# Wider weight pieces before the main loop, a resident last weight chunk, and coupled remainders in an attention + GLU block on one Trainium2 core

## The chip, the cores and the metric

The kernel runs on one core of a Trainium2 chip (trn2). The metric is the device time of one launch in microseconds (us). Engines are named as the profile names them: PE multiplies matrices (PEld is its weight load), DVE, ACT and POOL work on rows of elements, SP issues the DMAs. Each engine works through its own queue in order; engines wait for each other by semaphores.

## What is computed

One transformer block on 2048 rows of 512 numbers: a layer norm with a modulation computed from `c`, attention with 32 heads of 16 numbers that share one key and one value head, a second modulated norm, and a gated linear unit with 1792 hidden columns. Cut to what matters:

```python
mod = (silu(c) @ w_mod).reshape(1, 6, 1, -1)          # sa, ca, ga, sb, cb, gb
h = layernorm(x) * (1 + ca) + sa
q = h @ wq  (32 heads of 16);  k = h @ wk;  v = h @ wv    # one k and v for all heads
p = softmax(q k^T / 4);  x = x + ga * ((p v) @ wo)
h = layernorm(x) * (1 + cb) + sb
x = x + gb * ((sigmoid(h @ w_gate) * (h @ w_up)) @ w_down)
```

## The kernel before

**Numbers.** Most products are made from float16 pairs: a value is split into a high part and the rest, and a product is three passes (high x high, high x low, low x high). So every weight has to be read as float32, scaled, and split into two float16 halves before it is used.

**Three stages in time.** First a prologue, whose order is the hand-written list `PLAN` (a token is one small step: `a` is one score tile for the row maxima, `x` its reduction on DVE, `q` a part of a query projection, `jb` one "beat" of the weight jobs, `mx`, `mn`, `mz` the end of unit 0's row maxima). Then a main loop of 32 units of 16 steps; a unit is 128 query rows and 16 heads, and two units make one block of 128 rows (16 blocks). Last a tail with what of the feed-forward part is left over, which runs with full 128x128 matmuls and whose order a scheduler sets.

**A step of the main loop** is two half-steps. Each issues in a fixed order two transposed score tiles (`st`, whose exponential ACT writes to `P`), two score tiles for the row maxima of a unit ahead (`sa`, reduced by DVE to `mx`), one part of P times V (`craw`), and then one piece of feed-forward or query work (`piece`, pieces of some terms). All these matmuls use a quarter of the columns and half of the rows of the array (64*32); eight of them at different places run side by side. A *term* here is 8 such matmuls, two row halves times four column groups; a term of 512 columns does the work of one full 128x128 matmul.

**Feed-forward groups of a block**, in terms: the output projection `wo` (12), three pairs of gate and up of 512 hidden columns each (24 a pair), the last 256 hidden columns, gate and up together (`rest`, 12), and the down projection (42): 138. There are two ways to run a group on the two row halves:

- `Halves`: each row half of the contraction goes into a bank of its own; at the end DVE reads one bank, ACT the other, and POOL adds them.
- `Couple`: two groups share the array, each on one row half, and change sides in the middle. Each ends as one whole sum in one bank. At the change PE waits until the half that was issued before is done (`take_over`; a tiny `nought` matmul in `hand_over` counts it).

Before the change the three pairs are Couples, and `wo`, `rest` and `down` are Halves.

**Order of the groups.** When block b's units end, `wo` of block b is put into `urgent` with a first step (`SKIP` 9 steps into the next unit, `SKIP0` 5 for the first block), and `pairs[0]`, the `down` of the block before, `pairs[1]`, `pairs[2]`, `rest` into `work`. `pick` takes the next group that is ready, `pace` says how many terms a half-step gets (2 to 3), `places` spreads them.

**Weights.** Gate and up weights are split once, kept in HBM (`wD`, the last chunk in `wD1`) and read back for every block as tiles of 512 KB (`gw`, `GWB` = 7 buffers, two DMAs a tile, 14 tiles a block). `ask` puts a tile's two loads into a list when a buffer has been spent, and `drip` issues one of them, or one of the waiting transposes, each half-step. The down weights stay on chip.

Splitting is done in two places. Five of the seven chunks are split in the prologue by 20 jobs: `job_load` reads a piece of 256 KB, `job_beat` makes the two halves (two activations on ACT, one subtraction on POOL) and stores the result of two beats ago in two DMAs, and then loads the piece of two beats ahead (four pieces in flight). The rest is split in the main loop (`weight_jobs`, 26 pieces, each three operations on POOL behind a load), over the first 52 steps.

**Row maxima.** A unit's score rows are shifted by their maximum. The chain is `m` (DVE) to `mm` (ACT, then DVE) to `mt` (DVE), out to HBM and back into rows of `qp` (`mD`), and only then can the unit's first `st` run. In the prologue this chain is unit 0's.

Of the kernel before, what the change touches and what calls it, by code (L numbers as in the profile page):

```python
# [16 lines left out]
P = 128  # L17
# [46 lines left out]
SKIP, SKIP0 = 9, 5  # L64
# [25 lines left out]
GWB = 7  # L90
# [4 lines left out]
NGW = 4 * NPR + 2  # L95
JCH = 5
# [3 lines left out]
def adaln_mqa_glu_kernel(  # L100
# [649 lines left out]
    def recip(b, o, lD, rD):  # L750
# [16 lines left out]
        defer(W2 if b else 1, recip2)  # L767
# [44 lines left out]
    wD1 = dr.tile([2, P, 2, 4, 256], F16, name="wD1")  # L812
    CH = [*range(2, NCH), 0, 1]
# [6 lines left out]

    def weight_jobs():
        jobs = []
        gw = {}

        def gate_up(i, kk, m):
            if m == 0:
                gw[i, kk] = gw_tile()
            g_ = gw[i, kk].rearrange("p m (k n) -> p k m n", k=2)

            def store():  # L830
                for k in range(2):
                    dst = wD[i // 2, 2 * kk + k, :, :, i % 2 * 256:(i % 2 + 1) * 256] if i < 2 * NPR else wD1[kk, :, k]
                    sp1.dma_start(dst, g_[:, k])
                gw.pop((i, kk))
                if (i, kk) == (NCH - 1, 1):
                    ask(0)

            split_weight((w_gate, w_up)[m][2 * kk * P:2 * (kk + 1) * P, CH[i] * 256:(CH[i] + 1) * 256].rearrange("(k p) n -> p k n", p=P),
                         g_[:, :, m], g_[:, :, 2 + m], [2, 256], store if m == 1 else None)

        for i in range(JCH, NCH):
            for kk in range(2):
                for m in range(2):
                    jobs.append(lambda i=i, m=m, kk=kk: gate_up(i, kk, m))
            if i == JCH:
                for k in range(4):
                    jobs.append(lambda k=k: split_weight(wo[k * P:(k + 1) * P, :], WO['woh'][:, k], WO['wol'][:, k], [D]))
        for k in FS:
            jobs.append(lambda k=k: split_weight(w_down[k * P:(k + 1) * P, :], wdh[:, k], wdl[:, k], [D]))
        return jobs  # L850
# [20 lines left out]
    def ask(spent):  # L871
        while use[0] < min(spent + GWB, NGW * NQ):
# [3 lines left out]
            src = wD[i // NDC, i % NDC] if i < NDC * NPR else wD1[i - NDC * NPR].rearrange("p k m n -> p (k m n)").rearrange("p (m n) -> p m n", n=512)  # L876
# [4 lines left out]
    def ffn_block(b):  # L881
# [38 lines left out]
        def wo_end(pa, pb):  # L920
# [64 lines left out]
        def last_begin():  # L985
            if tail:
                ask(at + NDC * NPR)
            fetched(at + NGW - 1)

        def last_term(n, rs):  # L990
            k, i = divmod(n, 3)
            gw = gws[at + NDC * NPR + k // 2].rearrange("p m n -> p (m n)")
# [4 lines left out]
        def last_end(pa, pb):  # L997
# [29 lines left out]
        def down_end(pa, pb):  # L1027
# [18 lines left out]
        first = Halves("wo", 12, "po", wo_term, wo_end, wo_alone, wo_begin)  # L1046
        pairs = [Couple(gu_pair(p, 0), gu_pair(p, 1)) for p in range(NPR)]
        rest = Halves("gu", 12, "pgu", last_term, last_end, last_alone, last_begin)
        down = Halves("dn", 3 * NFC, "pd", down_term, down_end, down_alone)
# [3 lines left out]
        for k in range(2):  # L1053
            rest.after[6 * k + 5] = lambda spent=at + NDC * NPR + k + 1: ask(spent)
        for g in (*pairs, rest):
            g.needs = [((b, "h2"), HGAP if b else EGAP)]
        down.needs = [((b, f"g{p}"), GAP) for p in range(NPR)] + [((b, f"g{NPR}"), -99)]
        return first, pairs, rest, down, norm_alone


    jobs, beat, wst = [(i, kk, m) for i in range(JCH) for kk in range(2) for m in range(2)], [0], {}

    def job_load(k):
        i, kk, m = jobs[k]
        if k == 0:
            wst["f"] = pro.tile([P, 4, D], F32, tag="xb", name="xb", bufs=4)
            wst["h"] = pro.tile([P, 4, 2, 2, 256], F16, tag="xb", name="xb", bufs=4)
        src = (w_gate, w_up)[m][2 * kk * P:2 * (kk + 1) * P, CH[i] * 256:(CH[i] + 1) * 256].rearrange("(k p) n -> p k n", p=P)
        sp1.dma_start(wst["f"][:, k % 4].rearrange("p (k n) -> p k n", k=2), src)

    def job_store(k):
        i, kk, m = jobs[k]
        for z in range(2):
            sp1.dma_start(wD[i // 2, 2 * kk + z].rearrange("p (e m) n -> p m e n", e=2)[:, m, :, i % 2 * 256:(i % 2 + 1) * 256],
                          wst["h"][:, k % 4, :, z])

    def job_beat():
        k, beat[0] = beat[0], beat[0] + 1
        if k < len(jobs):
            w_ = wst["f"][:, k % 4]  # L1080
            hi, lo = (wst["h"][:, k % 4, e].rearrange("p k n -> p (k n)") for e in range(2))
# [29 lines left out]
    def q_end(b, o):  # L1111
# [11 lines left out]
              "la": lambda: load_q(0, 0, 1), "lb": lambda: load_q(0, 1, 2), "jl": lambda: [job_load(k) for k in range(4)], "jb": job_beat}  # L1123
# [5 lines left out]
    downs, late = [], []  # L1129
# [7 lines left out]
    WO["wol"] = P2.tile([P, 4, D], F16, name="wol")  # L1137

# [49 lines left out]
    def pace(s, g):  # L1188
        if g.stage == "q":
            return QRATE, 2  # L1190
        now_, late_ = s // (NU * NKB), s % (NU * NKB) >= CHAIN
        until = 2 * ((now_ + late_) * NU * NKB + CHAIN)
        left = sum(z.n for z in [g, *urgent, *work] if late_ or z.b < now_ - 1 or z.stage == "wo") + 12 * late_
        if until > 2 * len(units) * NKB:
            until, left = 2 * len(units) * NKB, left - 12 * late_
        return min(max(LEAST, left / max(until - 2 * s, 1)), MOST), MOST
# [39 lines left out]
    for i, (b, o) in enumerate(units):  # L1236
        if o == 0 and b > 0:
            first_, pairs_, rest_, down_, _ = ffn_block(b - 1)
            first_.ready = i * NKB + (SKIP if b > 1 else SKIP0)
            urgent.append(first_)  # L1240
            block = [pairs_[0], *downs[-1:], *pairs_[1:], rest_]
            downs.append(down_)
            for g in (first_, *block):
                g.b = b - 1
# [59 lines left out]
    left = [*urgent, *work, downs[-1]]  # L1304
# [59 lines left out]
```

## Time and profile before

| | |
|---|---|
| runs | 1670.15, 1673.82, 1676.3 us; median 1673.82 |
| the profiled execution | 1675.08 us, span in the trace 1673.3 us |
| instructions | 92934 |
| PE, DVE, ACT, POOL busy | 1581.2, 1421.7, 1303.4, 685.6 us |
| granted PE clock, mean | 0.978 |
| read from and written to HBM | 160.23 and 20.56 MB |

The profile is of one execution. An engine's busy time is the union of its instructions; matmuls are pipelined, so their durations overlap and a busy PE is not PE at its peak. In rows of a timeline the columns are start, duration, engine, line, operation, result and operands, shape and count, and in square brackets how long the engine stood idle before it and what ended that. A table of waits has the total in us, the number of waits and the longest. In a table by stretches each engine has its busy time and the number of its instructions in brackets; then follow the granted clock, the share of time that the DMA engines were busy, and what they moved in GB/s. SPq is SP's queue: the time an issue took there.

### The profile page before, as it was taken

Reading aid. Unit: us, or ns where it says so; the run is one execution under the profiler, and the core shown is the slowest. Engines: PE = TensorE matmul, PEld = TensorE weight load, DVE = VectorE, ACT = ScalarE, POOL = GpSimd, SP = SyncE. Lnnn points to the kernel's source line nnn. Section 1 sums busy time; section 2 is a strip of 40 time slices with the busy share of each in tenths; the row PEclk is TensorE's granted clock in tenths of the full one; section 3 lists DMA queues with packets and bytes.
Section 4 is the critical chain, followed back from the end, with each engine's and each line's share of the span. In section 5 each row is a group of like instructions: output and inputs, shape, how many; then the busy total and the mean of one; then the engine's idle time right before and its main releaser. Section 6 shows DMA issues by size and latency. Waiting matters only on the chain.

```text
span 1673.3 us, 92934 instructions
## 1 busy us (share of the span) xinstructions
PE 1581.2 (94%) x41818; PEld 989.8 (59%) x41818; DVE 1421.7 (85%) x2410; ACT 1303.4 (78%) x2354; POOL 685.6 (41%) x824
## 2 busy tenths in 40 slices
PE   6868988999999999999999999999999999999998
PEld 3313544656666566666666666766666666666544
DVE  7548987989999999999999999999999999998031
ACT  4655876878888788888888888888888888888821
POOL 4542557634252525244352526252524435242510
PEclk9777999999999999999999999999999999999999
DMA  6473343642615325435373545454443636353553
GB/s 204 137 200 88 100 120 111 174 109 82 169 35 145 102 70 135 119 112 141 85 164 89 126 96 139 85 138 111 125 123 100 150 85 163 88 124 93 138 191 107
DMA packets 247482, 203.86 MB, mean 122 GB/s; under 512 B 126140, under 2 KB 178092, under 8 KB 247084
## 3 DMA queue, kind: packets, MB, share of 16 engines
q1 hardware_dynamic: 247084, 197.92, 44.6%
q8 instruction: 327, 5.36, 1.3%
q14 instruction: 71, 0.58, 0.1%
HBM read 160.23 MB, written 20.56 MB: 108 GB/s over the span
## 4 chain that ended last, share of the span: by engine, by line
PE 79%; DMA 6%; DVE 5%; ACT 5%; issue 2%; SPq 1%; POOL 1%; ACTq 0%; POOLq 0%; DVEq 0%
PE craw L146 22%; PE pgu L146 17%; PE sa L146 13%; PE st L146 12%; PE pd L146 7%; DVE mx L146 3%; ACT P L146 3%; PE po L146 2%; PE pd L266 2%; PE pq L146 2%; PE pgu L203 2%; DMA qp<-mD 1%; DMA xb<-in_B_w_up_dram 1%; SPq L146 1%; DMA mD<-mt 1%
## 5 line engine op out<-in xcount | busy, mean ns | idle before, releaser
L146 DVE TENSOR_REDUCE mx<-sa 128x1 f32<-128x512 f32 x2048 | 1293.2, 682 | 103.0 <-PE sa L146 86.3
L146 ACT ACTIVATE P<-st 128x512 f32<-128x512 f32 x2048 | 1166.7, 597 | 239.0 <-PE st L146 180.3
L146 PE MATMUL craw<-P,V 64*32 64x512 f32 x8192 | 1090.3, 595 | 0.8 <-issue 0.7
L146 PE MATMUL st<-qp,kp 64*32 64x512 f16 x8192 | 841.0, 380 | 19.6 <-ACT P L146 14.1
L146 PE MATMUL sa<-kp,qp 64*32 64x512 f16 (+1 forms) x7940 | 658.8, 380 | 35.9 <-DVE mx L146 33.5
L146 PEld LDWEIGHTS <-kp 64*32 64x32 f16 x8192 | 331.9, 91 | 279.4 <-issue 106.4
L146 PE MATMUL pgu<-gw,h 64*32 64x512 f16 x9600 | 427.8, 376 | 4.0 <-issue 2.4
L146 PEld LDWEIGHTS <-qp 64*32 64x32 f16 (+1 forms) x7940 | 259.5, 93 | 134.9 <-issue 73.2
L146 PEld LDWEIGHTS <-h 64*32 64x32 f16 (+1 forms) x9792 | 214.9, 92 | 84.2 <-issue 27.7
L146 PEld LDWEIGHTS craw<-P,V 64*32 64x32 f32 x8192 | 242.9, 105 | 23.0 <-issue 8.5
L146 PE MATMUL pd<-wdh,g 64*32 64x512 f16 x2912 | 150.2, 376 | 1.1 <-issue 0.8
L980 POOL TENSOR_SCALAR th<-th 128x512 f32<-128x512 f32 (+1 forms) x57 | 32.3, 566 | 276.5 <-ACT th L146 262.1
L146 PEld LDWEIGHTS <-g 64*32 64x32 f16 x4368 | 93.7, 92 | 32.9 <-issue 9.3
L1033 POOL TENSOR_TENSOR o<-o,gb 128x512 f32<-128x512 f32 x13 | 16.7, 1283 | 211.1 <-ACT o L146 211.1
L146 PE MATMUL pd<-wdl,g 64*32 64x512 f16 x1456 | 90.1, 376 | 1.8 <-issue 1.8
L609 POOL MEMSET qp<- 32x1024 f16 x60 | 56.7, 944 | 55.3 <-PE st L146 53.0
L981 POOL TENSOR_TENSOR th<-th,u 128x512 f32<-128x512 f32 (+1 forms) x57 | 65.3, 1146 | 4.7
L146 PE MATMUL po<-woh,a 64*32 64x512 f16 x960 | 59.4, 386 | 6.6 <-POOL a L774 6.6
L908 POOL TENSOR_TENSOR rows<-th,rows 128x512 f16<-128x512 f32 (+1 forms) x57 | 59.5, 1044 | 4.6
L146 PE MATMUL craw<-nought 64*32 64x1 f16 x336 | 54.8, 163 | 0.0
L146 DVE COPY u<-pgu 128x512 f32<-128x512 f32 x43 | 29.3, 681 | 26.6 <-PE pgu L146 19.1
L146 PE MATMUL pq<-h,wdh 64*32 64x512 f16 (+1 forms) x688 | 51.0, 388 | 0.0
(163 smaller groups left out, 1105.1 us busy)
## 6 DMA issues: line engine op xcount, KB each, us to landing
gw<-wD SPq DMA_DIRECT2D x448, 256.0 KB
wm<-in_w_mod_dram SPq DMA_DIRECT2D x6, 1024.0 KB
qp<-qD SPq DMA_DIRECT2D x186, 32.0 KB
wD<-xb SPq DMA_DIRECT2D x40, 128.0 KB
qD<-q SPq DMA_DIRECT2D x16, 256.0 KB
xr<-in_A_x_dram SPq DMA_DIRECT2D x16, 256.0 KB
out_dram<-ot SPq DMA_DIRECT2D x16, 256.0 KB
rD<-cs SPq DMA_DIRECT2D x124, 32.0 KB
```

The lines of the kernel that those rows point to most:

```text
L146: return (lambda *a, **k: keep(f_(*a, **k))) if pinned else f_
L203: pe.matmul(cut[0](self.bank) if cut else self.bank, l_, r_, start=(n == 0), stop=(n == self.n - 1))
L266: pe.matmul(self.bank, *self.term(n, slice(0, P)), start=(n == 0), stop=(n == self.n - 1))
L609: eng.memset(qp[j:j + 32], 0.0)
L908: pool.tensor_tensor(rows[:, n:2 * n], src, rows[:, :n], op=ALU.subtract)
L980: pool.tensor_scalar(th, th, 1.0, 1.0, op0=ALU.add, op1=ALU.mult)
L981: pool.tensor_tensor(th, th, u_, op=ALU.mult)
L1033: pool.tensor_tensor(o2, o2, mods[5], op=ALU.mult)
```

## The change

- **Prologue.** The weight jobs become 16 (`JP` = 2 pairs of 512 columns, four row blocks, gate and up) on pieces of 128 rows by 512 columns. A piece's rows are now 2 KB in the load, where they were 1 KB, and 1 KB in the store, where they were 512 B; a store is one DMA, where it was two. Eight pieces are in flight, loaded by `jl0` and `jl1` well ahead of the first beat, and a beat loads the piece of six beats ahead. The last beats come earlier in `PLAN`, ahead of `mx` and `mn`.
- **Main loop, weights.** It splits 30 pieces, where it was 26, over the same 52 steps. The last chunk's halves go to a tile that stays on chip (`gr`, the size of two `gw` tiles), so a block reads 12 tiles back, where it was 14; `GWB` is 6.
- **Groups.** From block 2 on `wo` is coupled with the `rest` of the block before. From block 6 on the `down`s of two blocks are coupled and run two blocks later; `rest` of block 0, `wo` of blocks 0 and 1 and `down` of blocks 0 to 5 stay Halves.
- **Pace.** `pace` spreads what is left evenly over all steps that are left, where it aimed at dates in each block.
- **First block.** `SKIP0` is 7, and the reciprocal of the first block's softmax sums is issued 3 steps after the load that it needs, where it was 1.

```diff
-SKIP, SKIP0 = 9, 5
+SKIP, SKIP0 = 9, 7
+PSOLO, DSOLO = 2, 6
-GWB = 7
+GWB = 6
-NGW = 4 * NPR + 2
-JCH = 5
+NGW = 4 * NPR
+JP = 2
...
-        defer(W2 if b else 1, recip2)
+        defer(W2, recip2)
...
+        def wo_end(po, second):
...
+            t1, xr = t32("t1"), x1["x"]
+            dve.tensor_tensor(t1, po, mods[2], op=ALU.mult)
+
+            def norm():
+                pool.tensor_tensor(xr, t1, xr, op=ALU.add)
+                defer(1, norm2)
...
+        def last_end(p_, second):
...
+            th, u_ = t32("th")[:, :256], t32("u")[:, :256]
+            act.activation(th, p_[:, :256], AF.Tanh, scale=0.5 / (SH * SW))
+            act.activation(u_, p_[:, 256:], AF.Identity)
+            gated(th, u_, NPR, 256)
...
+        def down_end(pd, second):
...
+            ot = t32("ot")
+            if second:
+                act.activation(ot, pd, AF.Identity)
+            else:
+                dve.tensor_tensor(ot, pd, mods[5], op=ALU.mult)
...
     def job_beat():
...
-        if k >= 2:
-            job_store(k - 2)
-            if k + 2 < len(jobs):
-                job_load(k + 2)
+        if n >= 2:
+            job_store(n - 2)
+            if n + 6 < len(jobs):
+                job_load(n + 6)
...
+    gr = P2.tile([P, 2, 2048], F16, name="gr")
...
     def pace(s, g):
...
-        now_, late_ = s // (NU * NKB), s % (NU * NKB) >= CHAIN
-        until = 2 * ((now_ + late_) * NU * NKB + CHAIN)
-        left = sum(z.n for z in [g, *urgent, *work] if late_ or z.b < now_ - 1 or z.stage == "wo") + 12 * late_
...
+        ahead = 138 * (NQ - 2 - s // (NU * NKB))
+        left = sum(z.n for z in [g, *urgent, *work]) + ahead
+        return min(max(LEAST, left / max(2 * len(units) * NKB - 2 * s, 1)), MOST), MOST
...
+            proj, pairs_, rest_, down_, _ = ffn_block(b - 1)
+            g = proj
+            if rests:
+                g = Couple(rests.pop(), proj)
+                g.stage = "wo"
...
+            if len(downs) == (1 if b - 1 <= DSOLO else 2):
+                d = downs[0] if len(downs) == 1 else Couple(*downs)
```

ACT's queue at the end of the prologue, before the change: `xb` is one activation of a weight job, `q_` the reading of a finished query projection, `mm` the step of unit 0's chain of row maxima that stands on ACT.

```order
L146 ACTIVATE xb<-xb 128x512 x2
L146 ACTIVATE q_1061<-pq 128x512
L146 ACTIVATE q_1060<-pq 128x512
L146 ACTIVATE xb<-xb 128x512 x12
L146 ACTIVATE q_1165<-pq 128x512
L146 ACTIVATE q_1164<-pq 128x512
L146 ACTIVATE xb<-xb 128x512 x8
L146 ACTIVATE mm<-m 128x16
```

The same place after it:

```order
L147 ACTIVATE xb<-xb 128x512 x2
L147 ACTIVATE q_1061<-pq 128x512
L147 ACTIVATE q_1060<-pq 128x512
L147 ACTIVATE xb<-xb 128x512 x10
L147 ACTIVATE q_1150<-pq 128x512
L147 ACTIVATE q_1149<-pq 128x512
L147 ACTIVATE mm<-m 128x16
```

Behind the first query evictions stood 20 activations of weight jobs ahead of `mm`; now 10 do, and none between the second evictions and `mm`.

SP's queue in the same stage, before: loads of pieces (`xb<-in_`), stores of results (`wD<-xb`, two DMAs each), and the store of a finished query projection (`qD<-q_`), which waits for POOL.

```order
L146 DMA wD<-xb 256x1x256 x2
L146 DMA xb<-in_B_w_up_dram 128x2x256
L146 DMA wD<-xb 256x1x256 x2
L146 DMA xb<-in_B_w_gate_dram 128x2x256
L591 DMA qD<-q_908 128x2x512
L146 DMA wD<-xb 256x1x256 x2
L146 DMA xb<-in_B_w_up_dram 128x2x256
```

After:

```order
L147 DMA wD<-xb 256x1x512
L147 DMA xb<-in_B_w_up_dram 128x512
L592 DMA qD<-q_914 128x2x512
L147 DMA wD<-xb 256x1x512
L147 DMA xb<-in_B_w_gate_dram 128x512
```

A store is one entry, where it was two, and a load that stands behind `qD<-q_` is now for the sixth beat after it, where it was for the second.

DVE's queue in the middle of the main loop, before, about one unit from the end of one block's pairs on: `u<-pgu` reads an up half, `th<-pgu` one of the two banks of `rest`, the others belong to the attention part.

```order
L146 COPY u<-pgu 128x512
L146 TENSOR_REDUCE mx<-sa 128x1 x8
L146 RECIPROCAL rc<-lc 128x16
L146 TENSOR_REDUCE mx<-sa 128x1 x6
L146 COPY th<-pgu 128x512
L146 TENSOR_REDUCE mx<-sa 128x1 x16
L146 TENSOR_REDUCE m<-mx 128x16
L146 TENSOR_REDUCE mx<-sa 128x1 x4
L146 SCALAR_TENSOR_TENSOR mm<-m,mm 128x16
```

The same stretch of a block after:

```order
L147 RECIPROCAL rc<-lc 128x16
L147 TENSOR_REDUCE mx<-sa 128x1 x6
L147 COPY u<-pgu 128x512
L147 TENSOR_REDUCE mx<-sa 128x1 x16
L147 TENSOR_REDUCE m<-mx 128x16
L147 TENSOR_REDUCE mx<-sa 128x1 x4
L147 SCALAR_TENSOR_TENSOR mm<-m,mm 128x16
L147 STREAM_TRANSPOSE mt<-mm 128x32
```

The copy `th<-pgu` of 512 columns is gone from DVE: 14 of them in the whole program before, 1 after. DVE loses 3 more reads of a `down` bank; ACT loses 13 reads of a `wo` bank and 4 of a `down` bank; POOL's additions of two halves go with them.

Counted over both programs, PE issues the same number of terms, but not at the same place: in the main loop 9600 matmuls into `pgu` and 4368 into `pd` before, 9408 and 4032 after (8 a term: 24 and 42 terms fewer), and the tail has 24 and 42 full matmuls more. Besides the last block and the `down` before it, which the tail does in both, the loop leaves it a `down`, two pairs and a `rest` before, and two `down`s, three pairs and a `rest` after. PE issues 10 more of the tiny `nought` matmuls.

More of the change, by code (lines that the diff above doesn't have):

```diff
@@ L811, in adaln_mqa_glu_kernel @@
     wD = dr.tile([NPR, NDC, P, 4, 512], F16, name="wD")
-    wD1 = dr.tile([2, P, 2, 4, 256], F16, name="wD1")
-    CH = [*range(2, NCH), 0, 1]
+    CH = [2, 3, 4, 5, 0, 1, 6]
     FS = [2 * c_ + e for c_ in CH for e in range(2)]
@@ L1063, in job_load @@
[L1063 to L1075, printed above, removed]
+        down.needs = [((b, f"g{p}"), GAP) for p in range(NPR)] + [((b, f"g{NPR}"), GAP)]
@@ new lines, in ffn_block, with job_load, job_store @@
+        return proj, pairs, rest, down, norm_alone
+    jobs, beat, wst = [(p, k, m) for p in range(JP) for k in range(NDC) for m in range(2)], [0], {}
+    def job_load(n):
+        p, k, m = jobs[n]
+        if n % 4 == 0 and n < 8:
+            wst[n // 4] = pro.tile([P, 4, D], F32, tag="xb", name="xb", bufs=4)
+        if n == 0:
+            wst["h"] = pro.tile([P, 4, 2, D], F16, tag="xb", name="xb", bufs=4)
+        sp1.dma_start(wst[n // 4 % 2][:, n % 4], gate_up_part(p, k, m))
+    def job_store(n):
+        p, k, m = jobs[n]
+        sp1.dma_start(wD[p, k].rearrange("p (e m) n -> p m e n", e=2)[:, m], wst["h"][:, n % 4])
@@ L1077, in job_beat @@
     def job_beat():
[L1078 to L1081, printed above, removed]
+        n, beat[0] = beat[0], beat[0] + 1
+        if n < len(jobs):
+            w_ = wst[n // 4 % 2][:, n % 4]
+            hi, lo = (wst["h"][:, n % 4, e] for e in range(2))
             act.activation(hi, w_, AF.Identity, scale=SW)
@@ L1303, in adaln_mqa_glu_kernel @@
     last_unit()
-    left = [*urgent, *work, downs[-1]]
+    left = [*urgent, *work]
     assert all(g.stage in ("gu", "dn") for g in left)
-    old = [g for g in left if g.stage == "dn"]
-    left = [g for g in left if g.stage == "gu"]
     def go_on(g):
@@ L1322, in adaln_mqa_glu_kernel @@
     late.clear()
-    for g in old[:-1]:
-        g.alone()
     norm_()
     go_on(pairs_[0])
-    old[-1].alone()
+    downs[0].alone()
     for g in pairs_[1:]:
```

118 lines of the change are left out of this document (69 added, 49 removed), and 14 rows, old and new, of the table PLAN.

## The prediction

> **What bounds the kernel now.** I read the busy times first, then the stretches, then the waits of the stretches that fall off. A stretch's columns are its length, PE, PEld, DVE, ACT, POOL, clock, DMA share and GB/s; the last row, of one tile's instructions, has PE, PEld and ACT alone.
>
> ```profile
> span 1673.3 us, 92934 instructions
> ...
> PE 1581.2 (94%) x41818; PEld 989.8 (59%) x41818; DVE 1421.7 (85%) x2410; ACT 1303.4 (78%) x2354; POOL 685.6 (41%) x824
> 80.00:100.00 20.00, 18.72 (x121) 6.28 (x118) 13.32 (x23) 13.49 (x24) 9.25 (x9) 0.91 0.78 221
> 110.00:130.00 20.00, 1.15 (x5) 0.31 (x5) 1.68 (x4) 10.86 (x19) 9.38 (x9) 0.58 0.79 223
> 800.00:1200.00 400.00, 393.66 (x11710) 263.44 (x11702) 377.10 (x634) 337.19 (x611) 164.75 (x191) 1.00 0.47 115
> 800.00:1200.00 400.00, 297.78 (x2248) 68.46 (x2248) 321.46 (x562) 1.00 0.47 115
> ```
>
> The middle of the loop is full: in 400 us PE works 393.7 and DVE 377.1, so both stand near the step time. The last row is the same stretch for the exponentials and their matmuls alone: 562 exponentials, four a step, are 140.5 steps of 2.85 us. The prologue has a hole: from 110 to 130 us PE works 1.15 of 20 us and DVE 1.68, while the DMA engines are busy 0.79 of the time. The waits from 84 to 150 us and the timeline say why:
>
> ```profile
> DVE mm L146 <- ACT mm L146: 18.3, 1, 18.3
> ```
>
> ```profile
> 97.71 0.57 SPq L146 DMA_DIRECT2D xb<-in_B_w_up_dram  x1
> 102.10 0.37 SPq L591 DMA_DIRECT2D qD<-q  x1
> ...
> 108.83 0.22 DVE L146 TENSOR_REDUCE m<-mx 128x16 f32<-128x64 f32 x1
> 127.19 1.29 ACT L146 ACTIVATE xb<-xb 128x512 f16<-128x512 f32 x2 [3.66 <-DMA xb<-in_B_w_up_dram]
> 128.38 0.20 ACT L146 ACTIVATE mm<-m 128x16 f16<-128x16 f32 x1
> 128.61 1.18 DVE L146 SCALAR_TENSOR_TENSOR mm<-m,mm 128x16 f16<-128x16 f32 x1 [18.28 <-ACT mm L146]
> 130.66 8.95 PE L146 MATMUL sa<-kp,qp 64*128 64x512 f16 x15 [19.51 <-DVE mx L146]
> 139.54 0.61 PE L146 MATMUL st<-qp,kp 64*32 64x512 f16 x4
> ```
>
> The row maximum `m` is there at 108.83 us. Its next step stands on ACT behind the last weight jobs, which wait for their loads, and runs at 128.38. DVE holds its queue for 18.28 us, PE runs out of score banks for 19.51 us. The loads are late because a beat asks only two beats ahead, and because SP stands for 3.8 us (98.28 to 102.10) before a query store, with a load behind it.
>
> **Step by step, against the profiled 1675.1 us.**
>
> *1. The hole in the prologue.* With 16 jobs, eight pieces loaded before the first beat and six in flight after it, the queue position of `mm` has no load near it. Two jobs keep ACT 2.46 us:
>
> ```profile
> 73.62 2.46 ACT L146 ACTIVATE xb<-xb 128x512 f16<-128x512 f32 x4
> ```
>
> From the first job at 73.6 us to 108.8 us are 35 us; 16 jobs need 19.7 us of ACT, and in the stretch from 80 to 100 us above ACT was busy 13.5 of 20 us with the jobs and all else: it fits. So I take 18.0 of the 18.28 us, 139.54 becoming about 121.5. Ends: -5 if ACT or the stores are still behind by 13 us, -22 if the smaller ACT waits before 109 us go too.
>
> *2. First block.* Around 240 to 285 us four stretches of 5 us have PE at 9.2 of 20 us, 10.8 us lost:
>
> ```profile
> 240.00:245.00 5.00, 1.64 (x29) 0.62 (x28) 2.21 (x5) 0.97 (x3) 2.97 (x4) 0.80 0.51 172
> 250.00:255.00 5.00, 1.58 (x37) 0.54 (x35) 1.18 (x2) 0.97 (x2) 4.59 (x7) 0.83 0.71 213
> 265.00:270.00 5.00, 2.74 (x69) 1.09 (x53) 3.44 (x7) 1.99 (x5) 4.83 (x7) 1.00 0.00 0
> 280.00:285.00 5.00, 3.25 (x96) 1.58 (x87) 3.28 (x7) 2.81 (x6) 0.00 (x0) 1.00 0.29 71
> DVE rc L146 <- DMA lc<-lD: 4.2, 1, 4.2
> PE po L146 <- POOL a L774: 3.4, 1, 3.4
> POOL wst L379 <- DMA wst<-in_B_w_down_dram: 25.0, 7, 7.3
> ```
>
> The 4.2 us on DVE goes: three steps of 2.85 us cover it. The wait of `po` stays, since its operand comes two steps later and so does `wo`. POOL's waits for pieces remain, with four pieces more. I take -6, the 4.2 and some 2 of what was late behind it; ends 0 and -10.8.
>
> *3. Terms that move.* The price of a term, from the page and from the middle of the loop:
>
> ```profile
> L146 PE MATMUL pgu<-gw,h 64*32 64x512 f16 x9600 | 427.8, 376 | 4.0 <-issue 2.4
> 855.64 0.66 PE L146 MATMUL pgu<-gw,h 64*32 64x512 f16 x16
> 856.94 0.66 PE L146 MATMUL pgu<-gw,h 64*32 64x512 f16 x16
> 858.24 0.40 PE L146 MATMUL pgu<-gw,h 64*32 64x512 f16 x5
> 858.28 0.16 PE L146 MATMUL craw<-nought 64*32 64x1 f16 x1
> 858.28 0.61 PE L146 MATMUL pgu<-gw,h 64*32 64x512 f16 x11
> 859.53 0.66 PE L146 MATMUL pgu<-gw,h 64*32 64x512 f16 x16
> ```
>
> A half-step with two terms (16 matmuls of 0.38 us, eight side by side), where nothing waits, is 1.30 us, so 2.60 a step; counted in the program's order a step has 4.3 terms in blocks 5 to 15 before. The tail prices a term:
>
> ```profile
> 1600.55 1.92 PE L146 MATMUL craw<-P,V 64*32 64x512 f32 x16
> 1644.87 5.34 PE L203 MATMUL pgu<-gw,h 128*128 128x512 f16 x24
> 1648.30 2.69 SPq L878 DMA_DIRECT2D gw<-wD x6
> 1650.05 0.60 PE L899 MATMUL pt<-ident,th 128*128 128x128 f32 x4
> 1650.49 5.34 PE L203 MATMUL pgu<-gw,h 128*128 128x512 f16 x24
> ```
>
> 24 matmuls from 1644.87 to 1650.05 are 0.216 us each. In the loop 66 terms fewer save 66 x 0.216 = 14.2 us where PE is the limit, nothing where DVE is. DVE is busy 94% here; I take -14 (ends 0, -15), since the quoted half-steps run at PE's own pace.
>
> *4. Evictions.* DVE loses 16 reads of a bank and ACT 17, all in the loop. The columns are busy time and ns of one:
>
> ```profile
> L146 DVE COPY th<-pgu 128x512 f32<-128x512 f32 x11 | 7.5, 680 | 0.0
> ```
>
> 16 x 0.68 = 10.9 us of DVE. Where PE is the limit they are hidden under it; I take half, -5 (ends 0, -11). ACT and POOL, less busy, count for nothing.
>
> *5. One buffer fewer.* A pair's last two tiles can only be asked for when the pair ahead has spent its first two: 15 terms before their use, seven half-steps of 1.4 us. `drip` sends one half tile a half-step, transposes first, so counted in the planner's order the worst tiles are issued two to five half-steps ahead (2.8 to 7 us), where it was seven. In the tail row above a load issued at 1648.30 is used from about 1652.4 without a wait, so it landed within 4.1 us. Most arrive in time; I take +3 in the loop (ends 0, and 14 blocks x 1.3 us short = +18).
>
> *6. Four pieces more, ten `nought`s more, more side changes.* POOL, busy 41%, hides the pieces, three operations each:
>
> ```profile
> 137.37 0.62 POOL L379 TENSOR_SCALAR wst<-wst 128x512 f32<-128x512 f32 x1
> 138.07 1.15 POOL L381 TENSOR_TENSOR gw<-wst,gw 128x512 f16<-128x512 f32 x1
> ```
>
> That is 4 x (0.62 + 0.62 + 1.15) = 10 us of its own; if one stands before a block's `a` it costs PE up to 2 us. The side change at 858.24 above costs nothing: the pieces start at 1.30, 1.30 and 1.29 us. I take +1, ends 0 and +5.
>
> [...] If each of the 16 new changes held PE for one matmul of 0.38 us, that would be +6; by the row it is 0, and the trace does not show the loss.
>
> *7. The tail.* It gets 66 matmuls: +14.2. Two pairs now follow each other with six buffers at two places; +1.5 (ends 0, +4).
>
> Sum: -18 - 6 - 14 - 5 + 3 + 1 + 15.7 = -23.3, so 1651.8 for the profiled execution. The median of the runs is 1.3 us under that execution: 1650.
>
> **Rivals.**
>
> *DVE is the limit.* Then item 3 gives nothing and item 4 all of its 10.9: +8, 1658. For it: DVE at 94% and 2.85 us a step, above PE's 2.60 plus 0.3 of a term. Against: the half-steps quoted, which run in step with PE.
>
> *The hole only shrinks.* ACT's queue is still behind when `m` comes, because a job's activation waits for the store that frees its half, and item 1 gives -5: 1663.
>
> [...]
>
> *The even pace smooths more.* A step has 2.85 - 2.60 - 0.07 (0.3 of a term) = 0.18 us of loss; over the 350 steps after block 5 that is 63 us, and a third of it is -20: 1630. For it: the old plan gave some half-steps three terms and some none. Against: most of that loss sits at the ends of units, which stay.
>
> *Slower: the buffer starves PE.* The last tiles of the third pair come late in every block; PE takes its queue in order, so scores and exponentials stand too. It decides where 14 blocks lose more than 23.3 us above the +3, 1.9 us each; a load that takes 5 us behind two transposes would do it: 1680. Against: SP serves 14% fewer loads, and a block has three places of other work between pairs.
>
> **Chances.** Forecast as it stands 0.55; DVE the limit 0.13; hole only shrinks 0.12; side changes 0.04; smoother 0.10; starved 0.06. A measurement of this kernel tells about 0.5% from no change, 8.4 us: faster below 1665.4. The shrunken hole lies just inside of that and is split, so faster 0.88, same 0.07, slower 0.05. The range reaches from the smoother case to the shrunken hole with a little above, 1630 to 1666; the forecast's own is 1641 to 1658.
>
> **What would show it.** Right: DVE's wait for `mm` under 3 us, the first `st` near 121 us; no DVE wait for `lc` in the first block; from the start of the last `craw` row to the span's end some 15 us more than now (1600.55 to 1673.3, 73 us); steps in the middle near 2.80 us; no `th<-pgu` copies on DVE. Wrong: PE waiting for `gw` loads in each block, steps that stay at 2.85 us, or ACT still waiting for `xb` when `m` is done.

## The result and the profile after

The changed kernel takes 1649.04 us (median of 4 runs, 1648.73 to 1649.9) beside 1674.84 us before: a ratio of 0.9851, 95% interval 0.9831 to 0.9872. Measured once more, it took 1648.20 us (median of 6 runs) beside 1668.85: 0.9884, interval 0.9864 to 0.9903. So it is faster by 1.2 to 1.5%, 20 to 26 us. The kernel before, measured beside each group of runs, took 1674 to 1676 us in four of five groups and 1668.85 in one; so runs of different groups are compared below by their ratios to it.

The page of the changed kernel, span and busy times:

```profile
span 1647.3 us, 91744 instructions
PE 1573.4 (96%) x41370; PEld 989.8 (60%) x41370; DVE 1412.0 (86%) x2396; ACT 1288.9 (78%) x2330; POOL 621.7 (38%) x777
```

The span is 26.0 us shorter. PE is busy 7.8 us less, DVE 9.7 less. For the rest I cut each trace at its exponentials: 64 activations `P<-st` are a unit, so the start of the first, the 129th and the 257th, and the end of the last, divide the span in five parts (us):

| kernel | first `P` | units 0-1 | units 2-3 | units 4-31 | tail |
|---|---|---|---|---|---|
| before | 140.2 | 87.5 | 101.3 | 1269.1 | 75.2 |
| changed | 120.6 | 87.2 | 95.9 | 1253.4 | 90.3 |
| changed, second profile | 122.2 | 88.4 | 97.8 | 1246.0 | 90.3 |
| short look-ahead | 128.2 | 88.0 | 96.6 | 1255.4 | 90.7 |
| look-ahead alone | 133.4 | 88.5 | 103.1 | 1266.4 | 75.2 |
| first block as before | 121.7 | 88.0 | 104.5 | 1255.4 | 90.3 |
| first block alone | 141.3 | 87.7 | 97.5 | 1266.9 | 74.9 |
| downs alone | 121.1 | 87.3 | 96.0 | 1248.2 | 87.0 |
| no couples | 120.4 | 87.7 | 95.2 | 1254.4 | 84.2 |
| old pace | 120.3 | 88.5 | 96.9 | 1276.6 | 84.8 |
| no loads late | 121.2 | 90.3 | 97.6 | 1226.2 | 89.7 |
| seven buffers | 121.6 | 88.1 | 97.5 | 1261.2 | 89.9 |
| narrow stores | 124.9 | 88.9 | 97.1 | 1261.7 | 90.9 |
| even pace alone | 140.6 | 88.0 | 103.2 | 1263.0 | 83.9 |

The two profiles of the changed kernel differ by 7.4 us in units 4 to 31. That column is therefore read only for differences above 8 us, or where the same units stand out in several traces.

The prologue after, the waits from 60 to 150 us and the timeline (start, duration, engine, what it writes and reads):

```profile
DVE mm L147 <- ACT mm L147: 0.6, 1, 0.6
ACT xb L147 <- DMA wD<-xb: 7.8, 5, 3.4
```

```profile
106.37 2.47 ACT L147 ACTIVATE xb<-xb 128x512 f16<-128x512 f32 x4 [3.39 <-DMA wD<-xb]
107.93 0.22 DVE L147 TENSOR_REDUCE m<-mx 128x16 f32<-128x64 f32 x1
...
109.70 0.22 ACT L147 ACTIVATE mm<-m 128x16 f16<-128x16 f32 x1
...
109.95 0.21 DVE L147 SCALAR_TENSOR_TENSOR mm<-m,mm 128x16 f16<-128x16 f32 x1 [0.61 <-ACT mm L147]
...
119.90 0.62 PE L147 MATMUL st<-qp,kp 64*32 64x512 f16 x4
...
120.61 0.60 ACT L147 ACTIVATE P<-st 128x512 f32<-128x512 f32 x1 [9.57 <-DMA wst<-in_B_w_up_dram]
```

The row maximum `m` comes at 107.93 us, as before (108.83). Its step on ACT follows at 109.70 instead of 128.38, DVE waits 0.6 us instead of 18.3, the first `st` runs at 119.90 instead of 139.54, and the first exponential starts 19.6 us earlier. ACT's weight jobs now wait for stores (`wD<-xb`), 7.8 us, not for loads. The last of these waits ends at 106.37 us, 1.6 us ahead of `m`.

The first block, waits from 205 to 300 us:

```profile
POOL wst L380 <- DMA wst<-in_B_w_down_dram: 17.3, 5, 6.5
POOL wst L380 <- DMA wst<-in_B_w_up_dram: 5.7, 1, 5.7
PE po L147 <- POOL a L776: 1.6, 1, 1.6
PE po L147 <- POOL a L775: 1.6, 1, 1.6
```

DVE's wait for `lc` is gone; PE's for `a`, 3.4 us, is 1.6 + 1.6; POOL still waits for its pieces.

The middle of the loop, exponentials and their matmuls alone, and the tail, last rows of `P,V` matmuls and the stretch from the last exponential on (columns as in the prediction):

```profile
800.00:1200.00 400.00, 303.20 (x2288) 66.83 (x2280) 326.25 (x572) 1.00 0.45 115
```

```profile
1559.44 1.92 PE L147 MATMUL craw<-P,V 64*32 64x512 f32 x16
```

```profile
1557.00:1647.30 90.30, 83.25 (x441) 38.98 (x434) 23.15 (x39) 10.21 (x20) 0.56 (x1) 1.00 0.34 118
```

572 exponentials are 143 steps of 2.80 us (2.85 before). From 1559.44 to the end are 87.9 us, 15.1 more than the 72.8 before, for 70 more matmuls in the tail stretch (441 against 371 before).

What I did not look for stands in the single units. Counted in the program's order, a unit of the second half before held 60 gate/up terms of 68, or 24 of 70, in turn. Since two `down`s are coupled into one group of 84 terms in every second block, the changed kernel has units that are nearly all `down` (unit 24: 2 gate/up terms of 64) and units that are all gate/up (unit 23: 68 of 68). Unit 23 before, units 22, 23, 24, 26 and 30 of the changed kernel:

```profile
1191.80:1238.10 46.30, 45.24 (x1339) 29.21 (x1327) 43.61 (x74) 38.73 (x72) 25.51 (x32) 1.00 0.49 138
```

```profile
1099.80:1146.90 47.10, 45.35 (x1324) 29.70 (x1309) 42.56 (x71) 38.15 (x71) 12.56 (x17) 1.00 0.51 131
1146.90:1195.10 48.20, 46.24 (x1343) 30.18 (x1335) 43.66 (x74) 38.55 (x70) 20.89 (x27) 1.00 0.57 150
1195.10:1237.00 41.90, 41.90 (x1292) 29.71 (x1286) 40.78 (x69) 36.60 (x67) 6.97 (x10) 1.00 0.18 45
1281.90:1329.00 47.10, 46.24 (x1344) 30.03 (x1332) 43.19 (x71) 37.58 (x69) 13.49 (x16) 1.00 0.63 169
1465.60:1513.80 48.20, 45.77 (x1303) 28.52 (x1298) 30.83 (x52) 38.58 (x70) 17.09 (x19) 1.00 0.66 169
```

A unit of `down`s takes 41.9 us with PE never idle and the DMA engines at 0.18; a unit of gate/up pairs takes 47 to 48 us, PE idle for 0.9 to 2.4 of them, at a DMA share of 0.5 to 0.66. The second profile has the same pattern in units 23 (48.7 us), 24 (42.3 us) and 30 (48.3 us), but its units 22 and 27 take 45.7 and 44.8 us, where the first has 47.1 and 48.5.

### The profile page after: what moved, and what is told of

It reads as the page before. It is cut to its first block, busy times and chain, and to the rows that moved or that the text cites. A ratio compares the mean times of both kernels' runs of the same rounds, so it can differ in the third digit from the quotient of the medians.

```text
span 1647.3 us, 91744 instructions
## 1 busy us (share of the span) xinstructions
PE 1573.4 (96%) x41370; PEld 989.8 (60%) x41370; DVE 1412.0 (86%) x2396; ACT 1288.9 (78%) x2330; POOL 621.7 (38%) x777
## 4 chain that ended last, share of the span: by engine, by line
PE 73%; DVE 7%; DMA 6%; POOL 4%; ACT 4%; issue 3%; SPq 2%; ACTq 0%; POOLq 0%; DVEq 0%
PE craw L147 20%; PE pgu L147 14%; PE sa L147 12%; PE st L147 12%; PE pd L147 6%; DVE mx L147 5%; PE pd L204 2%; PE po L147 2%; PE pgu L204 2%; SPq L147 2%; ACT P L147 2%; PE pq L147 1%; DMA gw<-wD 1%; DMA mD<-mt 1%; DMA qp<-mD 1%
## 5 line engine op out<-in xcount | busy, mean ns | idle before, releaser
L147 PE MATMUL st<-qp,kp 64*32 64x512 f16 x8192 | 838.0, 379 | 18.3 <-ACT P L147 8.4
L147 PEld LDWEIGHTS <-kp 64*32 64x32 f16 x8192 | 336.0, 91 | 281.5 <-issue 100.6
L147 PE MATMUL pgu<-gw,h 64*32 64x512 f16 x8064 | 358.4, 378 | 8.9 <-DMA gw<-wD 3.7
L147 PEld LDWEIGHTS <-h 64*32 64x32 f16 (+1 forms) x9600 | 216.1, 92 | 83.9 <-issue 32.8
L147 PE MATMUL pd<-wdh,g 64*32 64x512 f16 x2688 | 138.6, 376 | 0.4 <-issue 0.2
L147 PE MATMUL pgu<-gr,h 64*32 64x512 f16 x1344 | 101.5, 377 | 0.6 <-DVE ot L147 0.3
L774 POOL TENSOR_TENSOR raw<-raw 128x256 f32<-128x256 f32 x31 | 22.7, 732 | 210.2 <-DMA raw<-lD 210.2
L147 PEld LDWEIGHTS <-g 64*32 64x32 f16 x4032 | 86.2, 92 | 21.4 <-issue 3.1
L147 PE MATMUL po<-woh,a 64*32 64x512 f16 x960 | 82.0, 377 | 6.1 <-POOL a L775 3.1
L147 PE MATMUL pd<-wdl,g 64*32 64x512 f16 x1344 | 80.3, 376 | 0.0
```

Source lines behind the costliest of these rows:

```text
L147: return (lambda *a, **k: keep(f_(*a, **k))) if pinned else f_
L774: keep(pool.tensor_tensor(rw, rw, raw[:, 2 * QU:], op=ALU.mult))
```

## The experiments

### The prologue: look-ahead and store width

The first puts the short look-ahead back, the second gives the kernel before the deep one with its own 20 narrow pieces, the third splits the changed kernel's stores.

```diff
 short look-ahead (changed kernel; the second group of four loads is left out of the plan too)
-            if n + 6 < len(jobs):
-                job_load(n + 6)
+            if n + 2 < len(jobs):
+                job_load(n + 2)
 look-ahead alone (kernel before; two groups of four loads stand in the plan, as after the change)
+        if k % 4 == 0 and k < 8:
+            wst[k // 4] = pro.tile([P, 4, D], F32, tag="xb", name="xb", bufs=4)
...
-            if k + 2 < len(jobs):
-                job_load(k + 2)
+            if k + 6 < len(jobs):
+                job_load(k + 6)
 narrow stores (changed kernel)
-        sp1.dma_start(wD[p, k].rearrange(...)[:, m], wst["h"][:, n % 4])
+        for z in range(2):
+            z_ = slice(z * 256, z * 256 + 256)
+            sp1.dma_start(wD[p, k].rearrange(...)[:, m, :, z_], wst["h"][:, n % 4, :, z_])
```

> The changed kernel, but the weight jobs of the prologue have four pieces loaded ahead of the first beat and load two beats ahead, as before the change; 16 wide pieces, their stores and the place of the beats stay. Theory (the hole was the late loads: two beats of look-ahead, and loads that stand behind a query store on SP): the activations of the jobs wait for their loads again, mm is late by some 8 to 15 us, the first st at 129 to 136 us, whole time +8 to +15 us over the changed kernel's 1649. Rival (fewer and wider jobs that end earlier in the list are enough): the first st stays within 3 us of 120.6 us, whole time within 3 us of the changed kernel.

> The kernel before, with the deep look-ahead alone: eight of its narrow pieces are loaded early and each beat loads six beats ahead; the 20 jobs, their two-DMA stores and the late beats stay. Theory (late loads): DVE's wait for mm falls from 18.3 to under 5 us, the first st from 140.2 to 122 to 127 us, whole time -13 to -18 us. Rival (number and place of the jobs: 20 activations stand ahead of mm, and SP needs 1.9 us a beat): the hole shrinks by 5 us or less, first st at 135 us or later.

> The changed kernel with each of the 16 prologue stores split in two of 256 columns, so that rows are 512 bytes as before the change, and SP issues 16 DMAs more. Theory 1 (after the loads, the stores' narrow rows and number are what held the hole open: the deep look-ahead alone brought 6.8 of 19.6 us): DVE's wait for mm comes back with 4 to 12 us, the first score matmul moves from 120.6 to 124 to 131 us, total 1653 to 1659 us. Theory 2 (the four jobs fewer did it): wait under 2 us, first score at 120 to 122 us, total 1648 to 1651 us.

Short look-ahead: 1656.55 us, ratio 0.9904 (0.9869 to 0.9938); look-ahead alone: 1668.71 us, 0.9968 (0.9944 to 0.9991); narrow stores: 1659.12 us, 0.9908 (0.9878 to 0.9938). The waits from 60 to 150 us of the three, in this order:

```profile
ACT xb L147 <- DMA xb<-in_B_w_gate_dram: 7.9, 3, 2.9
ACT xb L147 <- DMA xb<-in_B_w_up_dram: 6.7, 4, 3.8
DVE mm L147 <- ACT mm L147: 4.2, 1, 4.2
```

```profile
DVE mm L146 <- ACT mm L146: 13.3, 1, 13.3
ACT xb L146 <- DMA wD<-xb: 13.1, 8, 3.7
```

```profile
ACT xb L147 <- DMA wD<-xb: 12.8, 7, 3.6
DVE mm L147 <- ACT mm L147: 4.1, 1, 4.1
```

Without the look-ahead ACT waits for loads again and the first exponential comes at 128.2 us, 6.0 to 7.6 us later than in the two profiles of the changed kernel; `mm` runs on ACT at 117.22 us, 7.5 us later, just under the 8 to 15 expected, and the rival, within 3 us, is out. With the look-ahead alone the loads are in time, but ACT now waits 13.1 us for stores, and of 18.3 us the wait for `mm` keeps 13.3: the first exponential comes only 6.8 us earlier. The wait shrinks by 5.0 us, as the rival expected, and the start of the scores lies between the two expectations. So the deep look-ahead is worth 6 to 8 us of the 18.0 to 19.6. Narrow stores bring the wait for `mm` back to 4.1 us and the first exponential to 124.9, that is 2.7 to 4.3 us later, the lower end of what Theory 1 expected. What is left, some 8 to 9 us, was not split: four jobs fewer (two jobs are 2.46 us of ACT, so four are 4.9), the wider loads and the earlier place of the last beats came together. The whole time of the narrow stores rose by more than the prologue; the rest, 8 to 16 us, is in units 4 to 31, where the edit changes nothing. Their profile is of the slowest of four runs (1665.27 us, median 1659.12), and this rest stays unexplained.

### The first block

```diff
 first block as before (changed kernel)
-SKIP, SKIP0 = 9, 7
+SKIP, SKIP0 = 9, 5
...
-        defer(W2, recip2)
+        defer(W2 if b else 1, recip2)
 first block alone (kernel before): the same lines the other way round
```

> The changed kernel with the first block's two dates as before: wo ready 5 steps into the unit, the reciprocal one step after its load. Theory: DVE waits some 4 us for lc again and units 2 and 3 together are 4 to 8 us longer than the 95.9 us of the changed kernel. Rival (the lighter start of the loop, with earlier gw loads, took that time out, not the dates): units 2 and 3 within 2 us of 95.9.

> The kernel before with the two new dates of the first block alone. Theory: no wait of DVE for lc, units 2 and 3 together (101.3 us before) 4 to 8 us shorter, whole time -4 to -8 us. Rival (the dates only move the waits): units 2 and 3 within 2 us of 101.3.

With the old dates the changed kernel takes 1659.99 us, 0.9917 (0.9891 to 0.9943), and units 2 and 3 grow by 6.7 to 8.6 us. The new dates alone, in the kernel before, give 1667.47 us, 0.9961 (0.9944 to 0.9978); units 2 and 3 shrink by 3.8. The waits of the first block, old dates in the changed kernel and new dates in the old one:

```profile
PE st L147 <- DMA qp<-mD: 7.2, 2, 5.8
PE po L147 <- POOL a L775: 2.7, 1, 2.7
DVE rc L147 <- DMA lc<-lD: 2.1, 1, 2.1
```

```profile
PE po L146 <- POOL a L774: 8.2, 1, 8.2
```

The wait for `lc` comes and goes with the dates: it is in neither profile with the new ones. PE's wait for the next unit's maxima (`qp<-mD`) goes with it: 1.9 us before the change and none after it in the stretch from 205 to 300 us. That the late `lc` is what delays the maxima is argued from DVE's order of work, not shown. In the old kernel the wait of `po` stays, as predicted, and even grows from 3.4 us. The gain of 3.8 us lies just under the 4 to 8 expected.

### Which part of the loop's change does what

```diff
 downs alone
-PSOLO, DSOLO = 2, 6
+PSOLO, DSOLO = 2, 99
 no couples
-PSOLO, DSOLO = 2, 6
+PSOLO, DSOLO = 99, 99
...
-    go_on(rests[0])
+    go_on(left.pop())
```

> The changed kernel, but every block's down stays alone, as in the first blocks: no two downs are coupled. Counted in the program's order, units of the second half then hold 23 to 57 gate/up terms each, where the changed kernel has units of 0 and 2 such terms beside units of 65 to 73 (22, 23, 26, 27, 30). 18 terms come back from the tail into the loop, and the down's second banks are read again. Theory 1 (gate/up pairs that stand back to back are what makes units 22, 23, 26, 27 and 30 last 47 to 48.5 us, more than the coupled downs save): units 20 to 29 go from a mean of 45.4 us to 44.4, the loop as a whole loses 8 to 14 us, 1636 to 1644 us in all. Theory 2 (coupling saves bank reads on DVE and ACT and the long units are only the other half of the short ones): the loop gains 0 to 8 us, the tail loses 4: 1648 to 1655 us.

> The changed kernel, but no output projection, rest or down of two blocks is coupled: all stay alone, with two banks each that are read separately. 30 terms come back into the loop from the tail. My fourth term (the reads of a bank saved by coupling are worth 5 us, 0 to 11) expects the loop to be 5 us plus 30 x 0.216 = 6.5 us longer and the tail 6.5 us shorter: about 1654 us. The theory that clustered gate/up pairs cost more than the reads save expects 1636 to 1646 us. The theory that the reads are hidden under PE and clusters cost nothing expects 1649 +- 2.

Downs alone: **1640.40 us** (1637.87 to 1642.13), 0.9799 (0.9775 to 0.9824). The interval lies below both of the changed kernel's: coupling the downs costs 9 to 14 us by these ratios, and a version without it beats both kernels by 2.0% and 0.5 to 0.9%. Its units 22 to 24 and 26:

```profile
1108.40:1152.80 44.40, 44.33 (x1342) 31.37 (x1327) 42.67 (x72) 38.18 (x69) 11.36 (x14) 1.00 0.41 110
1152.80:1197.70 44.90, 43.69 (x1312) 30.09 (x1311) 42.69 (x73) 37.67 (x71) 22.35 (x29) 1.00 0.37 90
1197.70:1240.90 43.20, 43.15 (x1314) 30.27 (x1306) 42.21 (x71) 37.33 (x68) 10.83 (x14) 1.00 0.52 129
1286.80:1332.50 45.70, 44.57 (x1330) 29.80 (x1314) 42.50 (x70) 37.88 (x69) 9.80 (x13) 1.00 0.53 121
```

47.1, 48.2, 41.9 and 47.1 (45.7, 48.7, 42.3 and 46.7 in the second profile) became 44.4, 44.9, 43.2 and 45.7: the short unit gained less than the long ones lost. In six profiles with coupled downs and the even pace, units 20 to 30 add up to 494.5 to 503.5 us, here to 489.5; units 10 to 19 take 449.0 here, 441.7 to 448.7 there. The time is as Theory 1 expected it (1636 to 1644), but the traces do not show its loop: in place of 8 to 14 us, units 4 to 31 are 5.2 us shorter than in the first profile of the changed kernel and 2.2 us longer than in the second, with 18 terms more in them (3.9 us at 0.216 each). The tail is 3.3 us shorter. PE's idle time in units 4 to 31 (length less busy time) is 26.6 us here, 27.1 and 23.8 there. So that the coupled downs cost time is shown by the runs; that the clustered pairs are the reason is argued from the single units.

No couples at all: 1650.82 us, 0.9861 (0.9821 to 0.9902). Against downs alone this takes the rest's and projection's couples away: units 4 to 31 are 6.2 us longer, of which 3 are 14 matmuls that come back from the tail (417 there against 431). The couples of rest and projection are thus worth about 3 us in the traces, less than two profiles of one kernel differ by, and 10 us by the medians, whose intervals just overlap. The profile is of the fastest of these runs (1643.68 us). The interval, 1644 to 1658 us, leaves room for the first and the third expectation, and for the upper end of the second: this run alone does not decide between them. This is the part in which DVE loses its copies of `th<-pgu`.

```diff
 old pace: changed kernel with the rule before, which aims at each block's own end
 even pace alone: kernel before with
+        ahead = 138 * (NQ - 2 - s // (NU * NKB))
+        left = sum(z.n for z in [g, *urgent, *work]) + ahead
```

> The changed kernel with the rule before that sets how many terms a half-step gets: it aims at finishing each block in its own time, in place of one even pace to the end. Units then hold 46 to 80 terms where the even pace has 54 to 73, and 24 terms come back from the tail (5 us). The even-pace rival of the prediction expects a loop that is 10 to 20 us longer: 1655 to 1665 us. My own working gave smoothing nothing: 1647 to 1652 us.

> The kernel before with one edit: the even pace to the end of the loop in place of the rule that aims at each block's own end. Its units then hold about 66 terms (the old rule gave 68 to 70), some 40 terms go to the tail. If the even pace is worth something by itself (the old pace in the changed kernel cost 19 us), the loop gets 15 to 25 us shorter and the time is 1655 to 1668 us. If it is only needed to go with coupled downs, whose blocks are heavy and light in turn, the loop gains no more than the terms' price (9 us) and the tail loses it: 1670 to 1678 us.

The old pace in the changed kernel takes 1668.06 us, 0.9959 (0.9941 to 0.9977); units 4 to 31 take 1276.6 us, 23 to 31 more. Both expectations were too low; the rival's was the nearer. With blocks that hold a `down` of 84 terms or none in turn, a rule that ends each block in its own time gives units of 46 to 80 terms. The even pace in the kernel before takes 1678.15 us, 1.0022 (0.9993 to 1.005): nothing is won, units 4 to 31 lose 6.1 us and the tail gets 8.7 (46 matmuls). So the even pace is no gain of its own; in the changed kernel it is worth 13 to 18 us by the ratios. That it takes back what the coupled downs would cost without it is argued: uncoupled downs were not run with the old pace.

### What the units of gate/up pairs wait for

```diff
 no loads late
             u = use[0]
+            if u >= 48:
+                gws[u] = gws[u - GWB]
+                use[0] += 1
+                continue
 seven buffers
-GWB = 6
+GWB = 7
...
-        return wp.tile(list(shape), F32, tag="f32", name=name, bufs=18)
+        return wp.tile(list(shape), F32, tag="f32", name=name, bufs=16)
```

> The changed kernel without the loads of gate/up weights from the fifth block on: the matmuls read the six buffers as they were last filled (so the products of these blocks are of other weights), everything else is as it was. It tells what the long units with back-to-back pairs wait for. If transfers are what slows them (loads that come late, or that hold up other transfers such as the fetch of instructions), units 13, 22, 23, 26, 27 and 30 fall from 46.5 to 48.5 us to 44 to 45.5 and the time to 1632 to 1642 us. If PE, DVE or ACT work of the pairs themselves is the limit, they stay within 0.5 us and the time within 4 us of 1649.

> The changed kernel with seven buffers of gate/up weights, as before the change (room for it is made by two fewer of the 18 general f32 buffers). It tells which transfer the long units wait for. If it is the gate/up loads themselves, which can be asked for too late where two pairs follow each other, the loop gets much of the 23 us back that leaving out the loads gave: units 22, 23, 26, 27 and 30 fall by 1.5 to 3 us each, total 1635 to 1643 us. If the loads only hold up others (instruction fetch, transposes), or PE's own pace counts, an earlier request changes little: 1646 to 1651 us.

Without the loads from the fifth block on: 1624.50 us, 0.9706 (0.968 to 0.9731), which is below the 1632 to 1642 expected. Units 4 to 31 take 1226.2 us, 20 to 27 less, and the long units are gone; here units 23 and 24 of this run, then of the run with seven buffers:

```profile
1141.00:1186.20 45.20, 45.10 (x1346) 30.47 (x1335) 43.08 (x74) 38.41 (x71) 20.96 (x27) 1.00 0.20 39
1186.20:1228.20 42.00, 42.00 (x1294) 29.37 (x1286) 40.91 (x69) 36.60 (x67) 6.96 (x10) 1.00 0.14 26
```

```profile
1156.90:1206.20 49.30, 46.56 (x1347) 29.73 (x1335) 43.79 (x74) 38.54 (x71) 21.05 (x27) 1.00 0.62 151
1206.20:1248.50 42.30, 42.30 (x1293) 29.57 (x1286) 40.81 (x69) 36.52 (x67) 6.97 (x10) 1.00 0.17 40
```

The same 1343 to 1347 matmuls of unit 23 take 45.2 us without loads and 48.2 to 49.3 with them; unit 24, which loads little, does not move. So the loads are what makes the long units long, by their issue or their traffic; the edit takes out both. But PE does not wait there for the arrival of the weights: with seven buffers, asked for earlier (and two general buffers fewer), the time is 1658.51 us, 0.9899 (0.9866 to 0.9932), no better than with six, and unit 23 is as long as it was. In the changed kernel PE's named waits for loads between 390 and 1557 us are small:

```profile
PE pgu L147 <- DMA gw<-wD: 3.7, 4, 1.8
PE st L147 <- issue: 3.4, 5, 2.3
PE pgu L147 <- issue: 2.6, 5, 1.0
```

With seven buffers, in the same stretch, no wait for `gw<-wD` is left, and waits for nothing named (`issue`) have grown in its place:

```profile
PE pgu L147 <- issue: 7.1, 7, 1.9
```

That leaves, as an inference, loads that hold up something else. One stall at the end of unit 27 (PE's timeline, SP's timeline just before it, and the DMA queues from 1358 to 1372 us with packets, MB and share):

```profile
1370.10 0.40 PE L147 MATMUL st<-qp,kp 64*32 64x512 f16 x4 [2.26 <-issue]
```

```profile
1359.95 4.66 SPq L147 DMA_DIRECT2D gw<-wD  x8
1367.46 0.58 SPq L147 DMA_DIRECT2D mD<-mt  x1
```

```profile
q1 hardware_dynamic: 3047, 2.81, 86.1%
q8 instruction: 3, 0.05, 2.0%
```

Eight loads of 256 KB go out in 4.7 us; PE then stands with nothing to wait for. Of `q8`, whose 323 packets of 16 KB in 1647 us (one in 5.1 us, 1.07 us long in the mean) are instructions, one packet starts at 1359.91 us and takes 1.93 us. The next starts only at 1367.52, 7.6 us later, where the two steps before it were 4.2 and 4.0 us, and PE goes on 1.5 us after that one's end.

To see whether this is more than one case, I took all pauses in which PE starts no weight load for over 0.8 us, between 400 and 1600 us. In the fourteen profiles there are 415, whatever they wait for, and 174 of them (42%) end 1.0 to 1.5 us after the end of a 16 KB packet; these half microseconds cover 11% of the time, so about 46 would do so by chance. In the two profiles of the changed kernel it is 15 of 32 and 11 of 22, without the loads 1 of 15. PE's idle time in units 4 to 31 falls from 27.1 and 23.8 us to 12.8 without the loads, that is by 11 to 14 of the 20 to 27 us. The rest is time that the trace counts as busy, for the same matmuls, and is not explained.

The packets themselves hardly get longer: in the two profiles of the changed kernel, between 400 and 1600 us, those of 16 KB take 1.12 us in the mean where the loads' queue fills over 0.6 of the DMA engines, 1.05 us where it fills under 0.1. That they are behind the pauses is made likely by the times above, not shown: no run changed these packets and left the loads.

### The changed kernel again

> The changed kernel itself once more, in five rounds. Five runs with the same work in the loop (look-ahead short, first block old, seven buffers, narrow stores) agree on units 20 to 30 within 2.6 us of the mean (498 to 504 us), but have 448 to 449 us in units 10 to 19 where the changed kernel's one profile had 443. If that one profile was the lucky one, it now shows 446 to 450 us there and the time is 1651 to 1657 us; then the downs left alone gain 11 to 16 us, not 9, and narrow stores and seven buffers cost 2 to 8, not 10. If 1649 is its time, units 10 to 19 are 441 to 445 us and the time is 1647 to 1651 us; then those two edits really cost the loop 5 us or more.

1648.20 us (1646.51 to 1652.79), with 441.7 us in units 10 to 19 and 494.5 in units 20 to 30. The first profile was not a lucky one. But the two differ by 6.7 us in units 20 to 30 with one and the same program, so of the longer loops with seven buffers and narrow stores only this can be said: they are not shorter.

## Why the prediction was right, step by step

The forecast was 1650 us, 23.3 us less on the profiled execution; its span fell by 26.0.

*1, the hole (-18).* Measured -19.6, and -18.0 in the second profile. The place and the price were right. The cause that I gave, late loads, is 6 to 8 us of it; stores of narrow rows are another 3 to 4. The rest was not split: four jobs fewer are 4.9 us of ACT by the forecast's own price, and wider loads and earlier beats came with them. So the size was forecast better than its parts. ACT does wait for stores after the change, as the rival "the hole only shrinks" had it, but with 16 wide jobs these waits, 7.8 us, are over 1.6 us before `m` comes.

*2, the first block (-6).* -5.4 and -3.5 in the two profiles, and 3.8 to 8.6 in the runs that undo it or do it alone. Not foreseen: units 4 to 9 take 265.8 us where they took 272.7. They take 265.2 to 265.6 in the runs with the short and with the lone look-ahead too, 276.2 with the first block's dates alone and 270.4 with the even pace alone. So the gain seems to go with the prologue's jobs; it is as small as the spread between profiles, and what carries it was not traced.

*3 and 7, terms moved (-14 and +15.7).* The tail grew by 15.1 us. The even pace alone moves 46 matmuls and changes the time by nothing that can be measured. The two terms cancel, as the sum had it; the saving in the loop was not measured by itself.

*4, evictions (-5).* DVE is busy 9.7 us less, near the 10.9 worked out. What that is worth was split by the runs: the couples of rest and projection give some 3 us in the traces, with a difference of the medians that the intervals do not bear out, and the couples of the downs cost more than they save. One `th<-pgu` copy is left on DVE, that of the block that stays alone.

*5, one buffer fewer (+3).* PE waits 3.7 us for loads by name, where before it had no such wait. A seventh buffer takes these waits away and the time does not fall, so as a cost the term is not shown; the rival in which the buffer starves PE fell.

*6, side changes (+1).* Not tried by itself: no run changed their number alone. Six us spread over the loop's 448 steps of 28 units would be 0.01 us a step, too little to be seen in the 2.80 us that were forecast and measured, so neither 1 nor 6 us is ruled out.

*What the sum missed.* The order. I priced each coupled `down` by the reads it saves and moved terms by their number, and did not ask what stands in the place that the `down` leaves: gate/up pairs back to back, with their loads close together. Coupling the downs costs 9 to 14 us by the ratios; that these clusters are the reason is argued, as said above. For the loop items 3 to 6 gave -15, and units 4 to 31 are 15.7 us shorter in the first profile, 23.1 in the second; of that, 6.1 to 6.9 us are units 4 to 9, which no item foresaw. So that the loop came out so near is in part luck: a gain that was not counted stood against a cost that was not. The rival "the even pace smooths more" is refuted in its own form: alone it brings nothing. Its 13 to 18 us in the changed kernel (1668.06 with the old pace) look like a loss prevented.

## What to carry to other kernels

Before coupling work of two blocks to save reads, count per unit what each step loads: here, coupling the downs, which takes every second group that loads nothing from between groups that load much, cost 9 to 14 us by the ratios, with the reads it saved already taken off. Where a queue is late in a prologue, price the loads, the stores and the number of jobs each for itself: here, with the look-ahead alone, ACT waited 13.1 us for stores once its waits for loads were gone. And read single profiles of one program against each other before explaining a few microseconds between two.

## What the runs showed of the hardware that was not expected

- 42% of PE's pauses of over 0.8 us end 1.0 to 1.5 us after a 16 KB instruction packet, where 11% would by chance; without the late loads it is 1 of 15. That these packets cause them is not shown.
- Asking for weights earlier took PE's named waits for them away (3.7 us) and did not shorten the time: 1658.51 us with seven buffers.
- The loads cost the loop 20 to 27 us although PE's waits for them by name are 3.7 us.
